# Third gate group of a fused attention and two-MLP kernel: other buffers for its logits, and other steps for its load, clamp, exponential and logarithm

## The chip, the cores and the metric

The kernel runs on one core of a Trainium2 chip. The time is device microseconds of one execution; of several runs the median is given. The profile is one execution of its own, and times in it count from the first instruction of its span.

Engines are called TensorE (PE in the rows, its weight loads PEld), VectorE (DVE), ScalarE (ACT), GpSimd (POOL) and SyncE (SP). SyncE issues nearly all DMAs. Each engine works through its own instructions in order and waits for the others by semaphores.

## The reference

Three parts feed each other; all are float32.

```python
# 1: gated linear attention; batch 4, 8 heads, 768 positions, 48 per head
f = 1.0 / (1.0 + np.exp(-f_logit))
for t in range(S):
    state = f[:, :, t, :, None] * state + np.einsum('bhd,bhe->bhde', k[:, :, t], v[:, :, t])
    y[:, :, t] = np.einsum('bhd,bhde->bhe', q[:, :, t], state)
# 2: MLP on the 3072 tokens of 384 values, 2048 wide
h = x @ w_in
x = (h * (1.0 / (1.0 + np.exp(-h)))) @ w_out
# 3: 8 experts, one for each token, 1024 wide
logits = x @ w_gate
e = argmax(logits); gate_w = softmax(logits)[e]
out = gate_w * (np.maximum(x @ w1[e], 0.0) @ w2[e])
```

The inputs q, k and v are normal numbers times 0.1, f_logit is normal times 0.5 plus 2.

## The kernel before

**Chunks and groups.** The 3072 tokens are 24 chunks of 128, six to a batch. A chunk goes through the attention alone, with a state carried from chunk to chunk. Chunks make groups of 2, 2, 3, 3, 3, 3, 3, 3 and 2; a group goes through the first MLP together. Group 2 is chunks 4 to 6, group 3 is chunks 7 to 9.

**The gates of a group.** For each chunk the logits f are loaded ([128, 384] floats), clamped from below on VectorE (`f_step` 0), and turned into log(1 + exp(-f)) on ScalarE: an exponential (step 1) and a logarithm (step 2), in place. ScalarE needs another table of functions for the logarithm than for the exponential and for the tanh of the MLP, so it loads one ahead of the logarithm, and the pinned step `table` loads the old one back. From group 2 on, the logits of a whole group stand in one tile `in_f` of three chunks, with one buffer, and each of the three operations is one instruction over it (`f_group`). `att0(n)` casts a chunk's logarithms to two float32r parts, lfh and lfl, for groups whose `n` is 7 or more; a running sum over the chunk, `pl`, follows on TensorE.

**Steps.** The main loop runs over steps `s`, one for each block of 128 of the 2048 hidden columns of a group: `moe_h` (nine matmuls into ph, ScalarE's tanh se, VectorE's product sg), `moe_g` (high and low part, gh on ScalarE and gl on VectorE), and `moe_o` of two steps earlier (matmuls with gh and gl into px, which hold a group's result). The steps of groups 0 and 1 are 0 to 31, those of group 2 begin at 32, of group 3 at 48. ph has two banks, so a step's ph needs the sg of two steps before. When a group is done, `moe_x2` copies px into tiles x2 (five buffers of 388 floats), first for group 0 in step 32 and group 1 in step 33. Those rows wait there for the expert choice and its scatter.

**The order written out by hand.** For steps 0 to 30 the list `STEPS` gives three strings a step: what goes ahead of `moe_h`, what goes between `moe_h` and `moe_g`, and what goes behind `moe_o`. These names are mapped to functions by `do`; for the first 31 steps every instruction that they issue is pinned to this order on its engine. Behind that, a scheduler orders instructions.

The names that matter here:

- `li`, `lo`: load a block of w_in or w_out; `ci0` to `ci2`, `co0` to `co2`: three VectorE operations that make float32 numbers of the float64 that is loaded (cv); `hi`, `ho` and `Li`, `Lo`: its high part on ScalarE and its low part on VectorE. The two sets are about six steps ahead of the step that needs them.
- `f`: load of a chunk's logits; `fclamp`, `fexp`, `flog`: `f_group` of a group; `table`: the other table back.
- `fk`, `fq`, `kt`, `qt`: transposes of k and q on TensorE and their copies, on ScalarE for chunks below 7; `sc`: the scores; `am`: their mask, on VectorE; `past`, `own`: the parts of y from the earlier state and from the chunk itself; `pu`, `st`: the state; `y`: y's copy from PSUM.
- `yd`: `y_turn`. Chunks 4, 5 and 6 (`TURN`) leave y turned; three DMAs write it to DRAM, and one reads it back in the form that the MLP takes. All four are issued by SyncE one behind the other, so the last waits for the landing of the first three. `xh`, `xl` read the tile y.

The other pieces of the kernel, from chunk 7 on, are put at slots by a plan (`plan`, `after`): `att0(7)`, `att0(8)`, `att0(9)` at steps 27, 32 and 37, the load of the next group's logits at step 41.

Of the kernel before, what the change touches and what calls it, by code (L numbers as in the profile page):

```python
# [9 lines left out]
F32 = mybir.dt.float32  # L10
# [11 lines left out]
P = 128  # L22
CAP = 512
ROW = 388
# [90 lines left out]
def kernel(  # L115
# [15 lines left out]
    B, H, S, D = q.shape  # L131
    NT, DM = out.shape
    DFF = moe_w_in.shape[1]
    E, _, F2 = moe2_w1.shape
    KC = DM // P
# [7 lines left out]
    sizes = [2, 2] + [CPG] * ((NCH - 6) // CPG) + [2]  # L143
    NG = len(sizes)
    starts = [sum(sizes[:g]) for g in range(NG)]
# [13 lines left out]
    att = phase.enter_context(tc.tile_pool(name="att", bufs=1))  # L159
# [5 lines left out]
    ends = dram.tile([NCH, DM], F32, name="ends")  # L165
    xs = dram.tile([E * CAP, ROW], F32, name="xs")
    ys = {n: dram.tile([NPR * P, P], F32, name=f"ys_{n}") for n in TURN}
# [22 lines left out]
    def turned(n):  # L190
        return n > 6 or n in TURN
# [11 lines left out]
        return dict(tag=other, bufs=BUFS[other]) if n == 1 else dict(tag=own)  # L203

    fb = {}

    def load_chunk(n, names, pin=lambda fn: fn):
        b, c = divmod(n, CPB)
        g, r = group_of[n]
        for nm in names:  # L210
            src = {"f": f_logit, "q": q, "k": k, "v": v}[nm]
            if nm == "v":
                tag, bufs = ("gl", GB) if n == 1 else ("in_v", 1)
                flat = att.tile([P, H * D + 16], F32, tag=tag, name=f"v_{n}", bufs=bufs)
                if turned(n):
                    nc.gpsimd.memset(flat[:, H * D :], 0.0)
                t = flat[:, : H * D].rearrange("p (h d) -> p h d", h=H)
                loaded[nm, n] = flat
            elif n == 1:
                tag = {"f": "sg", "q": "gh", "k": "gh"}[nm]  # L220
                t = att.tile([P, H, D], F32, tag=tag, name=f"{nm}_{n}", bufs=BUFS[tag])
            elif nm == "f":
                if n in F_HOME:
                    fb[g] = att.tile([P, 1, H, D], F32, tag=F_HOME[n], name=f"f_{n}")
                elif n == starts[g]:
                    fb[g] = att.tile([P, CPG, H, D], F32, tag="in_f", name=f"f_{n}")
                t = fb[g][:, r if g > 1 else 0]
            else:
                t = att.tile([P, H, D], F32, tag="in_" + nm, name=f"{nm}_{n}")
            (pin(nc.sync.dma_start) if not strict else sy.dma_start)(out=t, in_=src[b, :, c * P : (c + 1) * P, :].rearrange("h p d -> p h d"))  # L230
            loaded.setdefault((nm, n), t)
# [13 lines left out]
    ve, ac, sy = Pinned(nc.vector), Pinned(nc.scalar), Pinned(nc.sync)  # L245
# [140 lines left out]
    am = {}  # L386
    ysb = {}
    xt = {}

    def f_step(t, k):  # L390
        if k == 0:
            ve.tensor_scalar_max(t, t, FMIN)
        elif k == 1:
            ac.activation(t, t, AF.Exp, scale=-1.0)
        else:
            ac.activation(t, t, AF.Ln, bias=1.0)

    def f_group(g, k):
        f_step(fb[g][:, : sizes[g]], k)

    def att0(n):
        f = loaded.pop(("f", n))
# [39 lines left out]
    def exps(n, nm):  # L442
        t = att.tile([P, H, D], F32, name=f"{nm}_{n}", **first_use(n, nm, "se"))
        scale = 1.0 if nm == "en" else -1.0
        ac.activation(t.rearrange("p h d -> p (h d)"), pls[n][:, :DM], AF.Exp, scale=scale)
        ee[nm, n] = t
# [10 lines left out]
    def put_ends(n, eng):  # L457
        ep2 = ee["ep", n].rearrange("p h d -> p (h d)")
        eng.dma_start(out=ends[n : n + 1, :], in_=ep2[P - 1 : P, :])
# [20 lines left out]
    def flat(n, nm):  # L480
        pads, i = (qpads, 1) if nm == "q" else (kpads, 2)
        p = use(n, i, f"p{nm}_{n}")
        for r in range(NPR):
            pe.transpose(
                p[:112, r * P : (r + 1) * P],
                pads[n % 2][:, 2 * r : 2 * r + 2, :].rearrange("p h d -> p (h d)")[:, :112],
                ident,
            )
        bd[nm, n] = p

    def unflat(n, nm):
        t = att.tile([112, NPR, P], F32, tag=nm + "t", name=f"{nm}t_{n}", bufs=2)
        p3 = bd.pop((nm, n))[:112, :].rearrange("p (r t) -> p r t", r=NPR)
        (nc.vector.tensor_copy if nm == "k" and n >= KACT else ac.copy)(t, p3)
        bd[nm + "t", n] = t
# [93 lines left out]

    def y_turn(n):  # L590
        yt = ysb[n]
        y = ysb[n] = att.tile([P, KC, P], F32, tag="y", name=f"y_{n}")
        if n in TURN:
            rows = ys[n].rearrange("(r p) t -> p r t", r=NPR)
            sy.dma_start(out=rows[:112, :2], in_=yt[:112, :2])
            for k in range(2):
                sy.dma_start(out=rows[64 * (1 - k) : 64 * (1 - k) + D, 2:], in_=yt[64 * k : 64 * k + D, 2:])
            sy.dma_start(out=y, in_=ys[n].rearrange("(h x) t -> h x t", h=H)[:, :D])
            return
        for h in range(H):  # L600
            r, j = divmod(h, 2)
            k = j ^ r // 2
            sy.dma_start(out=y[h * P // H : (h + 1) * P // H], in_=yt[64 * k : 64 * k + D, r])

    def att4(n):
        if n % CPB:
            y_past(n)
        y_own(n)
        if n % CPB < CPB - 1:
            gain(n)  # L610
        y_out(n)
        if turned(n):
            y_turn(n)
        if n % CPB < CPB - 1:
            carry(n, bd.pop(("pu", n)), n % CPB == 0)

    def carry(n, pu, first):
        pu3 = pu.rearrange("p (r e) -> p r e", r=NPR)
        ab = a_all[:112, n, :, None].to_broadcast([112, NPR, D])
        s = packed_state[:112, :, :D]  # L620
        if first:
            ve.tensor_tensor(out=s, in0=pu3, in1=ab, op=ALU.mult)
        else:
            ve.tensor_tensor(out=s, in0=pu3, in1=s, op=ALU.add)
            ve.tensor_tensor(out=s, in0=s, in1=ab, op=ALU.mult)
# [83 lines left out]
    x2 = {}  # L709
# [624 lines left out]
    for n in range(NCH):  # L1334
        g, r = group_of[n]
# [74 lines left out]
    def queue(early):  # L1410
        return ac if early else sy

    do = dict(
        f=lambda n: load_chunk(n, "f"), k=lambda n: load_chunk(n, "k"), q=lambda n: load_chunk(n, "q"),
        v=lambda n: load_chunk(n, "v"), clamp=lambda n: f_step(loaded["f", n], 0),
        exp=lambda n: f_step(loaded["f", n], 1), log=lambda n: (f_step(loaded["f", n], 2), set_f(n)),
        fclamp=lambda g: f_group(g, 0), fexp=lambda g: f_group(g, 1), flog=lambda g: f_group(g, 2), lf=set_f,
        table=lambda n: ac.preload_act_table_set("exp_and_others"),
        pl=sums, en=lambda n: exps(n, "en"), ep=lambda n: exps(n, "ep"), kmul=kmul, qmul=qmul,
        fk=lambda n: flat(n, "k"), fq=lambda n: flat(n, "q"), kt=lambda n: unflat(n, "k"), qt=lambda n: unflat(n, "q"),  # L1420
        sc=scores, am=mask, pu=gain, st=lambda n: carry(n, bd.pop(("pu", n)), n % CPB == 0), past=y_past, own=y_own,
        y=y_out, yd=y_turn, pt=flip_y, xh=x_high, xl=x_low,
        ends=lambda n: put_ends(n, queue(n == 0)), a=lambda n: spread_ends(n, queue(n == 0)),
        w=lambda n: warm(spare_bank[0], n),
    )
# [33 lines left out]
    g = NG - 1  # L1459
# [8 lines left out]
    def preload():  # L1468
# [6 lines left out]
        g=rest_fetch, t=lambda: turn(items["rest"]),  # L1475
# [50 lines left out]
```

## Time and profile before

| | before |
|---|---|
| median of 3 runs | 825.18 us (819.7 to 825.69) |
| the profiled execution's own time | 824.64 us |
| its span, first to last instruction | 822.9 us |
| TensorE busy | 799.7 us, 97% of the span |
| VectorE busy | 467.7 us, 57% |
| ScalarE busy | 379.1 us, 46% |
| mean granted clock of TensorE | 0.989 |

The profiled execution's time is 1.7 us longer than its span: what lies around the first and the last instruction. Shares of busy time are averages over the span; the stretch of the pinned steps looks otherwise, for example VectorE is busy for 4.93 of the 5 us from 95 to 100 us. Matmuls are pipelined and their ends are modelled, so a busy TensorE isn't TensorE at its peak.

### The profile page before, as it was taken

What the parts mean: (1) busy time and instruction counts of PE and PEld (TensorE: products, weight loads), DVE (VectorE), ACT (ScalarE), POOL (GpSimd) and SP (SyncE); (2) the same over time, 40 slices, a digit from 0 to 9 for tenths busy, and PEclk for the clock granted to TensorE, in tenths of its full rate; (3) what the DMA queues carried; (4) which work ended last, traced back from release to release, by engine and by line L of the source; (5) the groups of instructions that cost most, each with busy time, mean ns of one, the idle gap of its engine ahead of it and who ended that gap; (6) DMA issues with size and microseconds to landing.
All of it is one profiled execution on the core that took longest, in us unless ns stands there. A gap on an engine that the chain in (4) does not pass through costs nothing.

```text
span 822.9 us, 15636 instructions
## 1 busy us (share of the span) xinstructions
PE 799.7 (97%) x5831; PEld 750.0 (91%) x5831; DVE 467.7 (57%) x1258; ACT 379.1 (46%) x838; POOL 62.4 (8%) x114
## 2 busy tenths in 40 slices
PE   7999999999999999999999999999999999999994
PEld 4889979989999999999999999999899999989994
DVE  7789986555556555646656556366573426345520
ACT  5465564453453453454345342354473526445520
POOL 2000000001000100100100101001200010111001
PEclk9799999999999999999999999999999999999998
DMA  9566686424333343343443422323380617644500
GB/s 217 150 167 161 171 242 183 112 40 116 79 87 90 92 100 83 92 107 78 107 97 79 106 58 57 119 65 119 129 278 31 205 51 259 219 151 161 172 17 29
DMA packets 173197, 100.34 MB, mean 122 GB/s; under 512 B 115507, under 2 KB 166723, under 8 KB 173110
## 3 DMA queue, kind: packets, MB, share of 16 engines
q1 hardware_dynamic: 168724, 88.56, 39.4%
q0 software_dynamic: 3280, 9.49, 3.1%
q10 hardware_dynamic: 1106, 1.18, 0.4%
q8 instruction: 48, 0.79, 0.4%
q14 instruction: 39, 0.32, 0.1%
HBM read 79.35 MB, written 16.97 MB: 117 GB/s over the span
## 4 chain that ended last, share of the span: by engine, by line
PE 78%; issue 8%; DVE 7%; DMA 2%; ACT 2%; POOL 1%; SPq 1%; POOLq 0%; ACTq 0%; DVEq 0%
PE ph L420 22%; PE px L420 21%; PE p L420 8%; PE po L420 8%; PE py L420 4%; PE sc L420 2%; DVE out_cv L248 2%; PE pyb L420 2%; DVE in_cv L248 1%; PE plt L425 1%; PE pl L420 1%; PE p_r L420 1%; POOL out_dram L988 1%; PE pq L425 1%; PE pxs L425 1%
## 5 line engine op out<-in xcount | busy, mean ns | idle before, releaser
L420 PE MATMUL px<-out_lo,gh 128*128 128x384 f32 x368 | 130.2, 354 | 0.0
L679 DVE SCALAR_TENSOR_TENSOR sg<-se,ph 128x384 f32<-128x384 f32 (+1 forms) x113 | 60.2, 532 | 116.0 <-ACT se L677 114.9
L420 PE MATMUL ph<-xth,in_lo 128*128 128x384 f32 (+1 forms) x384 | 123.9, 323 | 0.7 <-DVE sg L679 0.5
L420 PE MATMUL px<-out_hi,gl 128*128 128x384 f32 x368 | 124.0, 337 | 0.0
L420 PE MATMUL ph<-xth,in_hi 128*128 128x384 f32 (+1 forms) x384 | 123.6, 322 | 0.0
L420 PE MATMUL ph<-xtl,in_hi 128*128 128x384 f32 (+1 forms) x384 | 122.3, 325 | 1.3 <-DVE sg L248 1.2
L420 PE MATMUL px<-out_hi,gh 128*128 128x384 f32 x368 | 123.4, 335 | 0.0
L677 ACT ACTIVATE se<-ph 128x384 f32<-128x384 f32 (+1 forms) x113 | 53.6, 474 | 137.1 <-PE ph L420 131.6
L687 ACT CAST gh<-sg 128x384 fp32r<-128x384 f32 (+1 forms) x113 | 56.3, 499 | 53.1 <-DVE sg L679 50.7
L688 DVE TENSOR_TENSOR gl<-sg,gh 128x384 fp32r<-128x384 f32 (+1 forms) x113 | 60.4, 535 | 25.8 <-ACT gh L687 25.1
L420 PEld LDWEIGHTS ph<-xtl,in_hi 128*128 128x128 f32 x384 | 71.7, 188 | 3.2 <-DVE sg L248 1.9
L420 PEld LDWEIGHTS ph<-xth,in_lo 128*128 128x128 f32 x384 | 72.2, 188 | 1.5 <-DVE sg L679 0.8
L420 PEld LDWEIGHTS ph<-xth,in_hi 128*128 128x128 f32 x384 | 72.1, 188 | 0.0
L420 PEld LDWEIGHTS px<-out_lo,gh 128*128 128x128 f32 x368 | 69.1, 188 | 2.5 <-ACT gh L687 0.6
L420 PEld LDWEIGHTS px<-out_hi,gl 128*128 128x128 f32 x368 | 69.3, 188 | 0.3
L420 PEld LDWEIGHTS px<-out_hi,gh 128*128 128x128 f32 x368 | 69.1, 188 | 0.0
L420 PE MATMUL po<-w_lo,hh 128*128 128x384 f32 (+4 forms) x184 | 62.9, 342 | 0.0
L420 PE MATMUL po<-w_hi,hh 128*128 128x384 f32 (+4 forms) x184 | 61.9, 336 | 0.0
L420 PE MATMUL po<-w_hi,hl 128*128 128x384 f32 (+4 forms) x184 | 61.9, 336 | 0.0
L276 DVE TENSOR_TENSOR w_lo<-w_raw,w_hi 128x384 fp32r<-128x384 f32 x104 | 52.3, 552 | 10.8 <-ACT w_hi L275 10.7
L420 PE MATMUL p<-xsl,w_hi 128*128 128x480 f32 (+6 forms) x168 | 58.4, 347 | 0.0
L420 PE MATMUL p<-xsh,w_hi 128*128 128x480 f32 (+6 forms) x168 | 58.3, 347 | 0.0
(290 smaller groups left out, 1532.6 us busy)
## 6 DMA issues: line engine op xcount, KB each, us to landing
w_raw<-in_moe_w_dram SPq DMA_DIRECT2D x64, 384.0 KB
xs<-big SPq DMA_DIRECT2D x8, 776.0 KB
in_again<-in_moe_w_in_dram SPq DMA_DIRECT2D x16, 384.0 KB
out_again<-in_moe_w_out_dram SPq DMA_DIRECT2D x16, 384.0 KB
in_raw<-in_moe_w_in_dram SPq DMA_DIRECT2D x15, 384.0 KB
xe<-xs SPq DMA_DIRECT2D x7, 776.0 KB
out_raw<-in_moe_w_out_dram SPq DMA_DIRECT2D x14, 384.0 KB
f<-in_f_logit_dram SPq DMA_DIRECT2D x24, 192.0 KB
```

The source lines that it names most:

```text
L248: return lambda *a, **k: tc.keep_in_program_order(fn(*a, **k))
L276: (keep(lo_engine.tensor_sub) if pin else lo_engine.tensor_sub)(lo[:, h], x, hi[:, h].bitcast(F32))
L420: ins = nc.tensor.matmul(*a, **k)
L425: ins = nc.tensor.transpose(*a, **k)
L677: ac.activation(e, ph[:, :GT], AF.Tanh, scale=0.5)
L679: ve.scalar_tensor_tensor(out=t, in0=e, scalar=1.0, in1=ph[:, :GT], op0=ALU.add, op1=ALU.mult)
L687: ac.copy(hi, t)
L688: ve.tensor_sub(lo, t, hi.bitcast(F32))
L988: ins = nc.gpsimd.indirect_dma_start(out=out[:, :], out_offset=bass.IndirectOffsetOnAxis(ap=idx[:n], axis=0), in_=o[:n], in_offset=None, b ...
```

## The change

- The loads of f_7, f_8 and f_9 go from step 18 to the end of step 5. Their tiles are no longer the group's `in_f` but three of the five x2 buffers, one tile a chunk.
- `fclamp:3` and `fexp:3` go from step 21 to step 7, `flog:3` and the `table` behind it from step 22 to step 8. `f_group(3, k)` is now three instructions, one for each chunk's tile, where it was one.
- `y_turn` is cut in two for chunks 4 to 6: the writes (`yd`) and the readback (`yb`, `y_back`). `yb` stands a step behind `yd`; `yd:5` moves from step 17 to 16, so that its readback keeps step 17.

```diff
-    ('co0:5 co1:5', 'co2:5 lo:7 ho:4 Lo:4 pt:3 xh:3 xl:3 st:3', ''),
+    ('co0:5 co1:5', 'co2:5 lo:7 ho:4 Lo:4 pt:3 xh:3 xl:3 st:3', 'f:7 f:8 f:9'),
     ('ci0:6 ci1:6', 'ci2:6 li:8 ho:5 Lo:5 pl:4 en:4 ep:4 kmul:4 qmul:4 ends:4 k:5 q:5', ''),
-    ('co0:6 co1:6', 'co2:6 lo:8 hi:6 Li:6', ''),
-    ('ci0:7 ci1:7', 'ci2:7 li:9 ho:6 Lo:6 fk:4 fq:4 kt:4 qt:4 a:4', ''),
+    ('co0:6 co1:6', 'co2:6 lo:8 hi:6 Li:6 fclamp:3', 'fexp:3'),
+    ('ci0:7 ci1:7', 'ci2:7 li:9 ho:6 Lo:6 fk:4 fq:4 kt:4 qt:4 a:4', 'flog:3 table:0'),
     ('co0:7 co1:7', 'co2:7 lo:9 hi:7 Li:7 sc:4 am:4', ''),
     ('ci0:8 ci1:8', 'past:4 ci2:8 li:10 ho:7 Lo:7', 'own:4 pu:4 y:4 v:5'),
     ('co0:8 co1:8', 'co2:8 lo:10 hi:8 Li:8 st:4 pl:5 en:5 ep:5 kmul:5 qmul:5 k:6 q:6 yd:4', ''),
-    ('ci0:9 ci1:9', 'ci2:9 li:11 ho:8 Lo:8', ''),
+    ('ci0:9 ci1:9', 'ci2:9 li:11 ho:8 Lo:8 yb:4', ''),
...
-    ('ci0:11 ci1:11', 'ci2:11 li:13 ho:10 Lo:10 xh:4 xl:4', ''),
-    ('co0:11 co1:11', 'co2:11 lo:13 hi:11 Li:11 pl:6 en:6 ep:6 kmul:6 qmul:6 ends:6 yd:5', ''),
-    ('ci0:12 ci1:12', 'ci2:12 li:14 ho:11 Lo:11 f:7 f:8 f:9', ''),
+    ('ci0:11 ci1:11', 'ci2:11 li:13 ho:10 Lo:10 xh:4 xl:4 yd:5', ''),
+    ('co0:11 co1:11', 'co2:11 lo:13 hi:11 Li:11 pl:6 en:6 ep:6 kmul:6 qmul:6 ends:6 yb:5', ''),
+    ('ci0:12 ci1:12', 'ci2:12 li:14 ho:11 Lo:11', ''),
...
-    ('co0:13 co1:13', 'co2:13 lo:15 hi:13 Li:13 sc:6 am:6 fclamp:3', 'fexp:3'),
-    ('ci0:14 ci1:14', 'ci2:14 ho:13 Lo:13 xh:5 xl:5', 'flog:3 table:0'),
+    ('co0:13 co1:13', 'co2:13 lo:15 hi:13 Li:13 sc:6 am:6', ''),
+    ('ci0:14 ci1:14', 'ci2:14 ho:13 Lo:13 xh:5 xl:5', ''),
     ('co0:14 co1:14', 'co2:14 hi:14 Li:14', ''),
     ('ci0:15 ci1:15', 'own:6 pu:6 y:6 ci2:15 ho:14 Lo:14', ''),
     ('co0:15 co1:15', 'co2:15 hi:15 Li:15 st:6 yd:6', ''),
-    ('', 'ho:15 Lo:15', ''),
+    ('', 'ho:15 Lo:15 yb:6', ''),
...
                 if n in F_HOME:
                     fb[g] = att.tile([P, 1, H, D], F32, tag=F_HOME[n], name=f"f_{n}")
+                elif g == 3:
+                    fx[n] = att.tile([P, ROW], F32, tag="x2", name=f"f_{n}", bufs=5)[:, :DM]
                 elif n == starts[g]:
                     fb[g] = att.tile([P, CPG, H, D], F32, tag="in_f", name=f"f_{n}")
-                t = fb[g][:, r if g > 1 else 0]
+                t = fx[n].rearrange("p (h d) -> p h d", h=H) if n in fx else fb[g][:, r if g > 1 else 0]
...
     def f_group(g, k):
-        f_step(fb[g][:, : sizes[g]], k)
+        for t in [fx[n] for n in range(starts[g], starts[g] + sizes[g])] if g == 3 else [fb[g][:, : sizes[g]]]:
+            f_step(t, k)
...
     def y_turn(n):
         yt = ysb[n]
-        y = ysb[n] = att.tile([P, KC, P], F32, tag="y", name=f"y_{n}")
         if n in TURN:
             rows = ys[n].rearrange("(r p) t -> p r t", r=NPR)
             sy.dma_start(out=rows[:112, :2], in_=yt[:112, :2])
             for k in range(2):
                 sy.dma_start(out=rows[64 * (1 - k) : 64 * (1 - k) + D, 2:], in_=yt[64 * k : 64 * k + D, 2:])
-            sy.dma_start(out=y, in_=ys[n].rearrange("(h x) t -> h x t", h=H)[:, :D])
             return
+        y = ysb[n] = att.tile([P, KC, P], F32, tag="y", name=f"y_{n}")
...
+    def y_back(n):
+        y = ysb[n] = att.tile([P, KC, P], F32, tag="y", name=f"y_{n}")
+        sy.dma_start(out=y, in_=ys[n].rearrange("(h x) t -> h x t", h=H)[:, :D])
```

## Rows read from the trace of the kernel before

**Rows 1.** The page, part 1: busy us (share of the span), instructions.

```profile
PE 799.7 (97%) x5831; PEld 750.0 (91%) x5831; DVE 467.7 (57%) x1258; ACT 379.1 (46%) x838; POOL 62.4 (8%) x114
```

**Rows 2.** Waits of VectorE, 28 to 135 us: us in total, times, longest.

```profile
DVE sg L248 <- ACT se L248: 9.4, 7, 2.6
```

**Rows 3.** Timeline of ScalarE, 98 to 126 us: start us, us, instruction.

```profile
107.90 1.17 ACT L248 ACTIVATE f<-f 128x1152 f32<-128x1152 f32 x1 [2.40 <-DVE f L248]
...
110.47 1.28 ACT L248 ACT_TABLE_LOAD   x1
111.77 1.17 ACT L248 ACTIVATE f<-f 128x1152 f32<-128x1152 f32 x1
112.95 1.28 ACT L248 ACT_TABLE_LOAD   x1
114.25 0.38 ACT L248 ACTIVATE se<-ph 128x256 f32<-128x256 f32 x1
```

**Rows 4.** Timeline of VectorE, 98 to 126 us; in brackets the idle time before.

```profile
107.12 0.75 DVE L248 TENSOR_SCALAR f<-f 128x1152 f32<-128x1152 f32 x1
107.78 0.42 DVE L248 TENSOR_TENSOR gl<-sg,gh 128x256 fp32r<-128x256 f32 x1
...
109.37 0.42 DVE L248 SCALAR_TENSOR_TENSOR sg<-se,ph 128x256 f32<-128x256 f32 x1 [0.31 <-ACT se L248]
...
114.66 0.42 DVE L248 SCALAR_TENSOR_TENSOR sg<-se,ph 128x256 f32<-128x256 f32 x1 [2.26 <-ACT se L248]
```

**Rows 5.** Timeline of TensorE, 107 to 125 us.

```profile
109.84 0.39 PE L420 MATMUL ph<-big,in_hi 128*128 128x256 f32 x1 [0.45 <-DVE sg L248]
...
115.14 0.38 PE L420 MATMUL ph<-xtl,in_hi 128*128 128x256 f32 x1 [1.24 <-DVE sg L248]
...
122.59 0.28 PE L420 MATMUL ph<-big,in_hi 128*128 128x256 f32 x1
...
124.70 0.28 PE L420 MATMUL ph<-xtl,in_hi 128*128 128x256 f32 x1
```

**Rows 6.** The tile f, its clamps in the pinned steps: duration ns min/median/max.

```profile
L248 DVE TENSOR_SCALAR f<-f x6: 349/356/753, 5.2 to 107.1; 128x384 f32<-128x384 f32 x4, 128x1152 f32<-128x1152 f32 x2
```

**Rows 7.** Timeline of ScalarE, 55 to 82 us.

```profile
58.16 0.50 ACT L248 ACTIVATE en<-pl 128x384 f32<-128x384 f32 x1
58.55 0.50 ACT L248 ACTIVATE ep<-pl 128x384 f32<-128x384 f32 x1
...
62.66 0.38 ACT L248 ACTIVATE se<-ph 128x256 f32<-128x256 f32 x1
...
63.81 0.61 ACT L248 COPY qt<-pq 112x512 f32<-112x512 f32 x1
```

**Rows 8.** Timeline of VectorE, 55 to 82 us.

```profile
63.16 0.42 DVE L248 TENSOR_TENSOR gl<-sg,gh 128x256 fp32r<-128x256 f32 x1
...
66.83 0.41 DVE L248 SCALAR_TENSOR_TENSOR sg<-se,ph 128x256 f32<-128x256 f32 x1
...
68.10 1.28 DVE L248 TENSOR_TENSOR am<-sc,trir 128x512 f32<-128x512 f32 x2
...
74.58 0.42 DVE L248 SCALAR_TENSOR_TENSOR sg<-se,ph 128x256 f32<-128x256 f32 x1 [1.54 <-ACT se L248]
```

**Rows 9.** Timeline of TensorE, 62 to 74 us.

```profile
65.17 1.16 PE L420 MATMUL sc<-qt,kt 48*128 48x128 f32 x16
...
68.84 0.43 PE L420 MATMUL py<-qt,state 48*64 48x128 f32 x4 [0.19 <-DVE am L248]
```

**Rows 10.** Timeline of SyncE, 48 to 126 us: DMAs that it issues.

```profile
55.80 0.35 SPq L248 DMA_DIRECT2D out_raw<-in_moe_w_out_dram  x1
...
100.16 3.72 SPq L248 DMA_DIRECT2D f<-in_f_logit_dram  x3
```

**Rows 11.** Engines in stretches: busy us (instructions), granted clock, DMA share, GB/s.

```profile
19.40:29.60 10.20, 10.15 (x60) 8.58 (x60) 4.54 (x10) 4.57 (x10) 0.00 (x0) 0.50 0.48 145
110.00:115.20 5.20, 3.96 (x48) 3.45 (x48) 2.90 (x8) 5.05 (x8) 0.41 (x1) 1.00 0.78 282
```

More of the change, by code (lines that the diff above doesn't have):

```diff
@@ L205 @@
     fb = {}
+    fx = {}
     def load_chunk(n, names, pin=lambda fn: fn):
@@ L1421 @@
         sc=scores, am=mask, pu=gain, st=lambda n: carry(n, bd.pop(("pu", n)), n % CPB == 0), past=y_past, own=y_own,
-        y=y_out, yd=y_turn, pt=flip_y, xh=x_high, xl=x_low,
+        y=y_out, yd=y_turn, yb=y_back, pt=flip_y, xh=x_high, xl=x_low,
         ends=lambda n: put_ends(n, queue(n == 0)), a=lambda n: spread_ends(n, queue(n == 0)),
```

## Prediction

> **What bounds the kernel now.** I read the page first: TensorE is busy for 97% of the span [rows 1], so no other engine can give back more than some per cent, and only where TensorE stands still. The change touches the first 31 steps, which run in a fixed order on every engine, so I read that stretch (about 30 to 130 us) alone: who VectorE waits for, then ScalarE, VectorE and TensorE in order of time. I number a step by its place in STEPS and count the activations se (one a step) to know which step a row belongs to. In this stretch VectorE, not TensorE, ends last most of the time: it does three conversion operations, a low part, sg and gl in each step and hardly rests. It rests for ScalarE's se, 9.4 us in seven waits [rows 2]; no wait in that answer names a DMA, so no load is late. Two of the seven belong to the group's logits.
>
> **The old place, steps 21 to 23.** VectorE runs the clamp at 107.12, 0.75 us, and its next operation starts at 107.78: 0.66 us spent. ScalarE then runs the exponential (1.17 us) ahead of that step's se, so VectorE rests 0.31 us before sg at 109.37. At the end of step 22 ScalarE loads a table, takes the logarithm and loads the table back, without a break between them: 110.47 to 114.23, 3.76 us, with the next se at 114.25 [rows 3]. VectorE rests 2.26 us for that se, to 114.66 [rows 4]. Together 0.66 + 0.31 + 2.26 = 3.23 us of VectorE's time.
>
> TensorE shows less, 0.45 us before 109.84 and 1.24 us before 115.14 [rows 5], 1.7 us in all. That isn't its whole loss: its three steps from 115.14 to the ph at 122.59 take 7.45 us, 2.48 each, by sg, while the next, without a wait, takes 2.11, to 124.70 [rows 5]. So VectorE decides until about step 27, and TensorE takes over there. If VectorE is 3.23 us earlier, TensorE's own work still fits: from the end of step 23's ph at about 107.8 to the ph at 122.59 it has nine blocks, each half of such a 2.11 us step (four ph, five px), and own and pu of chunk 6, by estimate 1.5 us, 11 us in all, which would end at 118.8; the last sg that it needs would be there at about 118.7, VectorE's 3.23 us earlier. Taking the work away gives back **3.2 us**; the bounds are 1.7 us (the visible rests alone) and 3.3 us.
>
> **The new place, steps 7 to 9.** The sequence stands at the same points: clamp in the middle of step 7 just ahead of gl, exponential at its end, logarithm and table at the end of step 8. It is now three tiles, so three instructions for one each time. A clamp of 128x384 takes 0.35 us against 0.75 for the large form [rows 6]; with VectorE's overlap, as above, three cost about 0.78 us against 0.66. Two 128x384 exponentials of another tile start 0.39 us apart [rows 7], so three take 1.17 us to the next start, against 1.07 from the large one. Splitting thus costs 0.1 us an operation, and lets the first exponential start after the first clamp, which gives 0.4 us back.
>
> Now ScalarE's chain, forward. The clamp takes the place of the gl at 63.16 [rows 8]; first clamp done 63.52, exponentials from 63.55, three times 0.39: se of step 8 at 64.72 instead of 62.66 [rows 7]. Behind it stand in this step what the old place hadn't: the copies kt and qt of chunk 4. qt begins 1.15 us after se, so 65.87, and ends at about 66.4 (0.61 us long, the next starts some 0.5 later); gh, 0.4 long, then to 66.8. Table 1.28, three logarithms 1.17 and the tail of the last some 0.15, table 1.28: 66.8 to 70.7. se of step 9 is at 70.74, sg 0.4 later at 71.14, as 114.25 and 114.66 stand to each other. VectorE alone would have come to that sg at 66.83 + 0.78 = 67.6, so it rests some 3 us here and about half a microsecond ahead of gl of step 8. The masks am of chunk 4 follow sg by 1.27 us [rows 8], at 72.41 instead of 68.10: **4.3 us late**.
>
> Who waits for that: TensorE's y of the earlier state in step 10. Before, it already waited for am by 0.19 us, at 68.84 [rows 9]; so am decides, and all that TensorE has behind it (px, own and pu of chunk 4, ph of step 11) comes 4.3 us later. That ph is what VectorE rests for at 74.58 (1.54 us) [rows 8], so no rest is left there to swallow the delay; both engines go on 4.3 us late. TensorE stands still for about 1.25 us ahead of the scores of step 9, which it began at 65.17 [rows 9] and which need qt, and, with the scores, px and ph between them, some 3.1 us ahead of the y. The trace of before doesn't show the sequence at this place. From the rows the cost lies between 1.7 us, the rests that the same sequence showed on TensorE at the old place, and 4.3 us; I take 4.3, because the row nearest to it, the y that waits for am, leaves no slack.
>
> **Loads and turns.** The three loads of f go from step 18 to step 5. Their buffers have had no user, so SyncE issues them at once behind the load at 55.80 (done at 56.15). In before they took 3.72 us to issue from 100.16 [rows 10], and VectorE read them at 107.12, 7.0 us after the first issue, without a wait; now it is 56.15 to 63.16, 7.0 us again. Hidden; at most some half a microsecond late. What they push back on SyncE (a load of an in piece, ends, k and q) is read four steps later or more. The three buffers belong to results that are first written at steps 32 and 33, after the casts of f_7 and f_8, and f_9 gives its buffer back at step 37, before the third group's results: no new wait.
>
> y_turn and y_back: SyncE now issues the readback of a turned chunk a step after the writes, so it needn't stand at their landing. Every piece keeps several steps of lead (the readbacks of steps 12, 17 and 26 are read in steps 16, 22 and 30), and no engine waits for a load, so I take nothing for it. The bounds are a gain of 0.3 us and a loss of 0.3 us, the order of the smaller rests seen here. The removed loads at step 18 free SyncE where no engine was waiting for it: nothing.
>
> **The sum.** 4.3 - 3.2 = +1.1 us on the profiled execution's 824.64: 825.7. The median of the runs is 0.5 us above that execution, so 826.
>
> **Rivals.**
> *The new rest is partly covered, slightly faster.* If TensorE is held only as long as it visibly was at the old place, 1.7 us: 824.64 + 1.7 - 3.2 = 823.1. If the 1.54 us that VectorE rests at 74.58 absorb a part: 824.2. For it: TensorE shows hardly a rest in this stretch, so it might run ahead. Against: the y waits for am already [rows 9], and TensorE works in order.
>
> *The clock falls, slower.* TensorE would stand still for 4.4 us of the 8.5 us from 65.2 to 73.7, and the matmuls of the y that end this rest are small. In before the granted clock fell to its lower level (0.50, 1.2 GHz) at 19.4 and stayed there to 29.6, after a stretch of small matmuls with rests; it stayed at 1.00 from 110.0 to 115.2 although TensorE was busy for only 3.96 of 5.2 us [rows 11]. My new rest is longer than the second case. If the clock falls at about 74 for as long as in the opening, 10.2 us, half of that is lost, 5.1 us, because TensorE is what ends last from there to step 11 and again from step 14: 825.7 + 5.1 = 830.8. If it comes back sooner, since large matmuls follow at once, some 828. It decides from the point where TensorE's rest ahead of the y is long enough for a 0.50 to show; with a rest as at the old place it doesn't.
> The Trainium skill (TensorE: Matmul & The Clock Gate, section "Why this matters for your kernels") warns against idle gaps between bursts of matmuls, since the clock drops back to half. It speaks against this change, as the row of the opening does; by that rule the time is the 830.8 of this rival, by the row of 110.0 to 115.2 it is 825.7.
>
> *The logits aren't there in time.* The change wouldn't do what it says if the load landed after 63.16; the clamp would hold VectorE, and am with it. The margin is that of before, so it costs 0 to 2 us: up to 827.7.
>
> **How the numbers follow.** The forecast, 824.5 to 827: 0.50. Covered, 822 to 824.5: 0.22. Clock, 827.5 to 831: 0.18. Late logits, or another order of the work after step 31, which isn't fixed: 0.10, on both sides. The range reaches from 821 (the covered case, and runs of before that lie up to 5.5 us under their median) to 831. About 1%, 8.3 us, is what a measurement of this kernel tells from no change (its three runs alone span 6 us); no case reaches it by itself, so faster by over 1% gets 0.04, slower 0.05, within 0.91.
>
> **What would show it.** In the changed kernel: no f instruction and no table load from 105 to 120 us, with sg at an even pace there (right), or a rest that stays (wrong). At 63 to 74 us: three clamps, three exponentials, two table loads around three logarithms; VectorE resting about 3 us for se of step 9; TensorE resting ahead of the scores and of the y. If that y comes at about 73, the 4.3 us stand; at 71 or earlier, I have overrated it. Granted clock 1.00 from 65 to 90 refutes the second rival. VectorE waiting for a DMA at the clamp would prove the third. I would be wrong in sign if the two places cost the same, which the copies kt and qt on ScalarE's path speak against.

## The result and the profile after

The changed kernel takes 826.96 us (median of 11 executions) where the kernel before, measured beside it, takes 820.94 us: ratio 1.0076, 95% interval 1.0056 to 1.0097. It is 6.0 us, 0.8%, slower. The forecast was 826 us, in a range of 821 to 831, and no change of more than 1%: the time came out in the range, but its effect was forecast as +1.1 us. The two don't go together because the sum started too high, from the profiled execution's 824.64 us. That execution is one of those whose granted clock fell in the opening, for 10.2 us [rows 11]; step 7 begins 5.1 us later in it than in the profile of the third experiment below, which has no such fall. In six of the nine profiles of the table below step 7 begins at about 55 us instead of 60 (two of the other three are late for a load at about 48 us, not for the opening), and the median of more executions of the kernel before is 820.94. One execution of all that follow, of the kernel with the sequence in steps 9 and 10, was slow, 874.35 us at a mean granted clock of 0.85, and its ratio leaves it out.

The profiled execution of the changed kernel takes 828.93 us, with a span of 827.1 us. The page, part 1, busy us and share of the span:

```profile
PE 800.4 (97%) x5831; PEld 750.6 (91%) x5831; DVE 468.3 (57%) x1260; ACT 379.2 (46%) x842; POOL 62.6 (8%) x114
```

Nothing shows there: TensorE has the same work as in [rows 1]. So the stretch of the pinned steps is read again, first the new place. ScalarE and VectorE, steps 7 to 9 (start us, us, instruction, in brackets the idle time before):

```profile
59.39 1.36 ACT L251 ACTIVATE f<-f 128x384 f32<-128x384 f32 x3 [0.80 <-DVE f L251]
60.65 0.36 ACT L251 ACTIVATE se<-ph 128x256 f32<-128x256 f32 x1
...
61.79 0.59 ACT L251 COPY qt<-pq 112x512 f32<-112x512 f32 x1
...
62.71 1.28 ACT L251 ACT_TABLE_LOAD   x1
64.00 1.35 ACT L251 ACTIVATE f<-f 128x384 f32<-128x384 f32 x3
65.37 1.28 ACT L251 ACT_TABLE_LOAD   x1
66.67 0.38 ACT L251 ACTIVATE se<-ph 128x256 f32<-128x256 f32 x1
```

```profile
59.00 0.89 DVE L251 TENSOR_SCALAR f<-f 128x384 f32<-128x384 f32 x3
...
67.08 0.42 DVE L251 SCALAR_TENSOR_TENSOR sg<-se,ph 128x256 f32<-128x256 f32 x1 [3.07 <-ACT se L251]
...
68.36 1.28 DVE L251 TENSOR_TENSOR am<-sc,trir 128x512 f32<-128x512 f32 x2
...
77.29 0.42 DVE L251 SCALAR_TENSOR_TENSOR sg<-se,ph 128x256 f32<-128x256 f32 x1 [3.99 <-ACT se L251]
```

Three clamps, three exponentials, the logarithms between two table loads, and kt and qt between them and the se of step 8, as forecast. Against [rows 7, 8] the masks am move from 1.27 us behind an undisturbed sg to 1.28 us behind one that waited 3.07 us. VectorE's rest ahead of the sg of step 11, 1.54 us in [rows 8], is now 3.99 us. TensorE:

```profile
62.44 1.16 PE L424 MATMUL sc<-qt,kt 48*128 48x128 f32 x16 [1.33 <-ACT qt L251]
...
69.10 0.69 PE L424 MATMUL py<-qt,state 48*64 48x128 f32 x4 [3.19 <-DVE am L251]
```

It rests 1.33 us ahead of the scores and 3.19 us ahead of the earlier-state y, where it rested 0.19 us in [rows 9]. The y starts at 69.10 us and not at the 73 of the forecast, but step 7 begins 4.1 us earlier in this execution: counted from step 7's se (56.09 here, 60.23 before) the y comes after 13.0 us instead of 8.6, so it is 4.4 us late. And from the end of that rest on the clock is low. Engines in stretches, TensorE's busy us first, the granted clock third from the end:

```profile
65.90:69.10 3.20, 0.01 (x2) 0.00 (x1) 2.02 (x5) 2.63 (x6) 0.00 (x0) 0.87 0.07 9
68.30:75.00 6.70, 5.90 (x44) 4.83 (x46) 4.93 (x12) 0.73 (x2) 0.00 (x0) 0.50 0.39 117
75.20:80.00 4.80, 4.80 (x42) 4.48 (x39) 2.68 (x7) 2.88 (x9) 0.11 (x1) 1.00 0.37 81
...
109.30:112.60 3.30, 3.30 (x14) 2.85 (x13) 2.26 (x6) 3.27 (x4) 0.00 (x0) 0.50 0.97 319
```

From 68.3 to 75.1 us it is 0.50, its lower level, and again from 109.2 to 112.6 us. The second belongs to the old place, which isn't empty. SyncE, VectorE, ScalarE and TensorE there:

```profile
96.85 1.28 SPq L233 DMA_DIRECT2D f<-in_f_logit_dram  x2
...
101.15 0.46 SPq L233 DMA_DIRECT2D f<-in_f_logit_dram  x1
```

```profile
106.31 0.76 DVE L395 TENSOR_SCALAR f<-f 128x1152 f32<-128x1152 f32 x1 [3.48 <-DMA f<-in_f_logit_dram]
...
111.48 0.43 DVE L251 TENSOR_TENSOR gl<-sg,gh 128x256 fp32r<-128x256 f32 x1 [1.01 <-ACT gh L251]
...
113.17 0.42 DVE L251 SCALAR_TENSOR_TENSOR sg<-se,ph 128x256 f32<-128x256 f32 x1 [0.41 <-ACT se L251]
```

```profile
107.10 1.16 ACT L397 ACTIVATE f<-f 128x1152 f32<-128x1152 f32 x1 [3.55 <-DVE f L395]
...
108.69 1.28 ACT L399 ACT_TABLE_LOAD   x1
109.98 1.16 ACT L399 ACTIVATE f<-f 128x1152 f32<-128x1152 f32 x1
...
111.46 1.28 ACT L251 ACT_TABLE_LOAD   x1
112.76 0.39 ACT L251 ACTIVATE se<-ph 128x256 f32<-128x256 f32 x1
```

```profile
108.39 0.45 PE L424 MATMUL spare<-out_hi,gl 128*128 128x384 f32 x1 [1.80 <-DVE gl L251]
...
116.12 0.45 PE L424 MATMUL spare<-out_hi,gl 128*128 128x384 f32 x1 [1.00 <-DVE gl L251]
```

The clamp, exponential and logarithm of a whole group stand here again, 1152 wide, but by their lines (L395, L397 and L399 instead of L251) they are not pinned, and their loads (L233) neither: they are the fourth group's, chunks 10 to 12. The tile f tells where they came from. Its clamps that aren't pinned, in before and in the changed kernel (first and last start in us):

```profile
L392 DVE TENSOR_SCALAR f<-f x5: 560/759/761, 161.4 to 429.5; 128x1152 f32<-128x1152 f32 x4, 128x768 f32<-128x768 f32 x1
```

```profile
L395 DVE TENSOR_SCALAR f<-f x5: 561/760/762, 106.3 to 434.3; 128x1152 f32<-128x1152 f32 x4, 128x768 f32<-128x768 f32 x1
```

The first of five moved from 161.4 us, in step 39, to 106.3 us, between the se of step 20 and that of step 21. The third group's logits used to keep the only buffer in_f until step 37. Now in_f is free as soon as the second group's sums are done, so the scheduler, which may place unpinned instructions among the pinned ones, put the fourth group's loads on SyncE at 96.85 us and its clamp on VectorE ahead of pinned work, and there VectorE stands 3.48 us for the load. VectorE's waits from 28 to 135 us, which named no DMA in [rows 2]:

```profile
DVE sg L251 <- ACT se L251: 13.0, 7, 4.0
DVE f L395 <- DMA f<-in_f_logit_dram: 3.5, 1, 3.5
```

### The profile page after: what moved, and what is told of

Read it like the earlier page. It is cut to its first block, busy times and chain, and to the rows that moved or that the text cites. A ratio compares the mean times of both kernels' runs of the same rounds, so it can differ in the third digit from the quotient of the medians.

```text
span 827.1 us, 15637 instructions
## 1 busy us (share of the span) xinstructions
PE 800.4 (97%) x5831; PEld 750.6 (91%) x5831; DVE 468.3 (57%) x1260; ACT 379.2 (46%) x842; POOL 62.6 (8%) x114
## 4 chain that ended last, share of the span: by engine, by line
PE 76%; issue 7%; DMA 6%; DVE 4%; ACT 3%; SPq 1%; POOL 1%; POOLq 0%; ACTq 0%; DVEq 0%
PE ph L424 22%; PE px L424 21%; PE po L424 7%; PE p L424 7%; PE py L424 4%; PE sc L424 3%; DMA w_raw<-in_moe_w_dram 2%; PE pyb L424 2%; PE pl L424 1%; PE spare L424 1%; DMA f<-in_f_logit_dram 1%; PE plt L429 1%; POOL out_dram L995 1%; PE p_r L424 1%; PE pq L429 1%
```

## The experiments

Ratios are to the kernel before, measured beside each of them; its medians there are 819.45 to 819.74 us, 1.2 to 1.5 us under the 820.94 above, so differences of medians from different experiments are good to a microsecond or two. A ratio is not simply the quotient of two medians. To see where time goes, I set the starts of se (one a step, ScalarE's timeline) of the profiled executions beside each other. The kernel of the third experiment serves as the measure: from step 5 to step 36 its profile runs 5.05 to 5.10 us ahead of before's, and it has no low clock in the opening. Each entry is the time between two starts, and the difference to that kernel in parentheses:

| kernel | step 7 to 11 | step 20 to 27 | span |
|---|---|---|---|
| before | 60.23 to 74.17: 13.94 | 100.47 to 122.24: 21.77 | 822.9 |
| before, split readback | 55.16 to 69.09: 13.93 | 95.39 to 117.14: 21.75 | 817.9 |
| changed | 56.09 to 76.87: 20.78 (+6.85) | 103.18 to 127.34: 24.16 (+2.41) | 827.1 |
| changed, fourth group pinned | 55.39 to 75.06: 19.67 (+5.74) | 101.35 to 119.69: 18.34 (-3.41) | 818.4 |
| changed, 20 matmuls | 55.09 to 73.44: 18.35 (+4.42) | 99.74 to 122.37: 22.63 (+0.88) | 819.8 |
| changed, 50 matmuls | 59.77 to 77.58: 17.81 (+3.88) | 103.89 to 126.39: 22.50 (+0.75) | 825.4 |
| changed, pinned and 50 matmuls | 54.61 to 72.94: 18.33 (+4.40) | 99.25 to 117.59: 18.34 (-3.41) | 816.6 |
| pinned, sequence in steps 9 and 10 | 60.73 to 77.00: 16.27 (+2.34) | 103.69 to 122.02: 18.33 (-3.42) | 820.8 |
| the same, later loads | 54.97 to 71.30: 16.33 (+2.40) | 98.00 to 116.34: 18.34 (-3.41) | 815.5 |

**The fourth group kept in program order.** The edit, in the changed kernel:

```diff
-                at(s0, load_chunk, m, "f")
+                at(s0, load_chunk, m, "f", *([keep] if g == 4 else []))
...
-    def f_step(t, k):
+    def f_step(t, k, pin=False):
+        hold = keep if pin else lambda fn: fn
         if k == 0:
-            ve.tensor_scalar_max(t, t, FMIN)
+            hold(ve.tensor_scalar_max)(t, t, FMIN)
...
-            f_step(t, k)
+            f_step(t, k, g == 4)
```

(The exponential and the logarithm likewise.) Expected:

> The changed kernel, with the load, clamp, exponential and logarithm of the fourth group (chunks 10 to 12) kept in program order, so that they can't move ahead into the pinned steps. Theory A, the freed buffer: the third group's logits left the one buffer in_f early, so the scheduler drew the fourth group's load, clamp and table loads into steps 20 to 22, where VectorE waited 3.5 us for the load. Then this kernel shows no f instruction from 100 to 130 us, the se of steps 20 and 27 keep or narrow their distance to before by 3.2 us instead of widening it by 2.4, and the time falls by about 4.7 us against the changed kernel, to 822 us. Theory B, the rest there comes of something else in the pinned order (the split readbacks, or TensorE's own work): the time stays at 826 to 827 us.

Measured: 820.76 us, ratio 0.9997 (0.9971 to 1.0024). VectorE has no f instruction from 100 to 130 us, and steps 20 to 27 give back 3.41 us where the changed kernel lost 2.41. Theory A holds, B falls: keeping one group's logits from moving ahead takes off 826.96 - 820.76 = 6.2 us by the medians. Program order puts the fourth group's clamp at 180.3 us, later than before's 161.4 us, so the edit does more than undo the move; the last experiment below shows what that alone is worth. The masks of step 9 and the clock are as they were: TensorE rests 3.2 us and the clock is 0.50 from 68.6 to 72.0 us in this profile.

```profile
PE py L425 <- DVE am L251: 3.5, 2, 3.2
PE sc L425 <- ACT qt L251: 2.1, 2, 1.3
```

```profile
65.20:68.50 3.30, 0.11 (x3) 0.11 (x4) 2.12 (x5) 2.62 (x6) 0.00 (x0) 1.00 0.10 12
68.60:71.90 3.30, 3.28 (x22) 2.49 (x18) 3.27 (x9) 0.40 (x1) 0.00 (x0) 0.50 0.29 106
72.00:80.00 8.00, 8.00 (x79) 7.53 (x78) 5.02 (x14) 3.30 (x10) 0.11 (x1) 1.00 0.55 147
```

**The buffers alone.** The kernel before with the x2 tiles and the three instructions, at the old steps. The edit is the lines of the change's diff that have to do with `fx` and `f_group`; STEPS and `y_turn` are as before.

> The kernel before with one part of the change alone: the third group's logits in three x2 buffers and three instructions for one, at their old steps 18, 21 and 22; y_turn as before. Theory A: the freed in_f alone draws the fourth group's logits into the pinned steps, so this kernel pays for both groups there, and is about 5 us slower than before (826 us), with an f instruction of 128x1152 between 95 and 110 us. Theory B: the buffers alone do nothing, 821 us as before.

Measured: 821.26 us, ratio 1.0019 (0.9987 to 1.0052), not to be told from before; the time is nearer to theory B's. The mechanism of theory A is there all the same, since VectorE runs both groups in the pinned steps:

```profile
93.11 0.75 DVE L395 TENSOR_SCALAR f<-f 128x1152 f32<-128x1152 f32 x1
...
98.22 0.43 DVE L251 TENSOR_TENSOR gl<-sg,gh 128x256 fp32r<-128x256 f32 x1 [1.82 <-ACT gh L251]
...
104.86 0.89 DVE L251 TENSOR_SCALAR f<-f 128x384 f32<-128x384 f32 x3
...
112.37 0.42 DVE L251 SCALAR_TENSOR_TENSOR sg<-se,ph 128x256 f32<-128x256 f32 x1 [2.46 <-ACT se L251]
```

but without a wait for a load, at a price of 3.15 us from step 17 (87.20 against 87.52 us) to step 27 (119.97 against 117.14), and 1.4 us of it come back later, in the profile between steps 39 and 42, where the fourth group's logits no longer stand. The 5 us were too much: I took them from the changed kernel, where the wait for the load and the low clock are in them.

**The readback alone.** The kernel before with `y_back` and the moved `yd` and `yb`; the edit is those lines of the change's diff and nothing else.

> The kernel before with the other part alone: the writes of the turned chunks and their readback apart by a step. No engine waits for these loads, so by the prediction's step it does nothing: within 0.3 us of before. If SyncE's stand at the landing had cost something, it is up to 1 us faster; if the readback of chunk 6 now comes too late, up to 1 us slower, with a rest of ScalarE ahead of xth at about 128 us.

Measured: 819.63 us, ratio 0.9981 (0.9947 to 1.0014). It does nothing that can be told, as forecast.

**Matmuls in TensorE's rest.** In the changed kernel, 20 matmuls with a constant operand ahead of the y of step 10, into columns 384 to 511 of a result bank, which nobody reads:

```diff
-    ('ci0:8 ci1:8', 'past:4 ci2:8 li:10 ho:7 Lo:7', 'own:4 pu:4 y:4 v:5'),
+    ('ci0:8 ci1:8', 'z:20 past:4 ci2:8 li:10 ho:7 Lo:7', 'own:4 pu:4 y:4 v:5'),
...
+        z=lambda n: [pe.matmul(px[0][0][:, DM:512], ones, ones, start=False, stop=False) for _ in range(n)],
```

> The changed kernel with 20 matmuls of 128 columns more on TensorE ahead of the earlier-state y of step 10, where TensorE rests 3.2 us for the masks am; their results land in columns of a result bank that nobody reads. Theory C, the clock: the rest lets the granted clock fall to 0.50 from 68 to 75 us, which costs 2.4 us; with the matmuls it stays at 1.00 there and the time is about 2.4 us less, 824.5 us. Rival: the steps after 10 are late for the masks alone; the clock may stay up, but the time stays at 827 us or grows by what the matmuls take beyond the rest.

Measured: 825.9 us, ratio 1.0062 (1.0026 to 1.0098), between the two expectations and by its median undecided, since the executions lie between 820.77 and 832.18: four with a mean granted clock of 0.993 or more take 823.2 us or less, eight with 0.991 or less take 825.3 us or more. The profiled one is of the first kind; its clock is 1.00 from 15 to 135 us, and it loses 4.42 us from step 7 to 11, not 6.85. Twenty matmuls leave 2.1 us of the rest, so the next two experiments took 50.

**Both.** The pinned fourth group and 50 matmuls:

> The changed kernel with both: the fourth group's logits kept in program order, and 50 matmuls of 128 columns (20 in the run before) ahead of the earlier-state y of step 10, whose results nobody reads. Theory C, the clock: the granted clock stays at 1.00 from 60 to 80 us, step 7 to step 11 loses 4.4 us instead of the 5.7 that it lost with the pinned group alone, and the executions whose clock doesn't fall in the opening are 1.3 us faster than that kernel's, 818.5 us. Rival: the matmuls take as much as the clock did: 820 us.

Measured: 818.13 us, ratio 0.9969 (0.9947 to 0.9991), 0.3% under before. Steps 7 to 11 lose 4.40 us. TensorE at the place of the rest, and the clock there:

```profile
60.95 1.16 PE L425 MATMUL sc<-qt,kt 48*128 48x128 f32 x16 [1.34 <-ACT qt L251]
...
64.26 2.96 PE L425 MATMUL px<-ones 128*128 128x128 bf16 x50
67.62 0.44 PE L425 MATMUL py<-qt,state 48*64 48x128 f32 x4 [0.39 <-DVE am L251]
```

```profile
64.80:68.00 3.20, 2.81 (x48) 2.44 (x45) 2.40 (x5) 2.25 (x6) 0.00 (x0) 1.00 0.14 31
68.00:75.00 7.00, 6.84 (x75) 6.04 (x74) 5.38 (x14) 2.91 (x8) 0.11 (x1) 1.00 0.44 129
```

Between this kernel and the one with the pinned group alone lie 1.34 us of these steps by the profiles (5.74 and 4.40) and 2.6 us by the medians. The mean granted clock of the executions says the same: 0.994 or more in ten of twelve here, in one of twelve there. The rival falls. That the kernel is now faster than before isn't due to the change alone: the kernel before with the same group pinned (the last experiment) takes 819.08 us, ratio 0.9983, and the two intervals overlap. What is left, 4.4 us, is the wait for am itself: the matmuls are done in the rest and the y comes no sooner.

**The 50 matmuls alone.** The changed kernel without the pinning:

> The changed kernel with the 50 matmuls ahead of the earlier-state y of step 10 and nothing else: the fourth group's logits move ahead as in the changed kernel. Against the kernel with both edits it shows what the freed buffer costs when the clock is held at the new place: theory A says steps 20 to 27 lose 0.9 to 2.4 us where that one gains 3.4, less about 1 us that comes back behind step 32, so 821.5 to 823.5 us against its 818.1. Against the changed kernel it shows what the clock at the new place costs by the median: 3 to 5 us. Rival: the clock falls at the other rest, for the fourth group's load at about 105 us, in most executions anyway, and the median stays over 825.

Measured: 823.34 us, ratio 1.0045 (1.0015 to 1.0074). The time is in theory A's range, and the rival falls. Against the changed kernel the matmuls are worth 826.96 - 823.34 = 3.6 us by the medians, 2.5 us by the ratios, whose intervals overlap. Not all of that lies at the new place: in the profiles steps 7 to 11 lose 3.88 us instead of 6.85, and steps 20 to 27 lose 0.75 us instead of 2.41; there the clock doesn't fall a second time, and the load is waited for more briefly. The fourth group's logits cost 823.34 - 818.13 = 5.2 us with the clock held, of which 0.75 + 3.41 = 4.2 us show in steps 20 to 27. VectorE waits for their load for 1.8 us in this profile, 3.5 us in the changed kernel's:

```profile
DVE f L395 <- DMA f<-in_f_logit_dram: 1.8, 1, 1.8
```

The profiled execution takes 827.11 us, more than the median, because TensorE waits 2.0 us for v of chunk 3 in it, to 47.6 us, and the clock is at 0.50 from 48.8 to 55.6 us.

**Another place, beside the second group's.** Loads in step 2, clamp, exponential and logarithm in step 4, where the second group's logarithm stands:

```diff
-    ('am:3 co0:4 co1:4', 'past:3 co2:4 li:7 ho:3 Lo:3 xh:2 xl:2', 'flog:2 table:0 lf:4 lf:5 lf:6 own:3 pu:3 y:3 v:4'),
+    ('am:3 co0:4 co1:4', 'past:3 co2:4 li:7 ho:3 Lo:3 xh:2 xl:2 fclamp:3', 'fexp:3 flog:2 flog:3 table:0 lf:4 lf:5 lf:6 own:3 pu:3 y:3 v:4'),
```

> The changed kernel with the fourth group kept in program order and the third group's sequence beside the second's: loads at the end of step 2, clamp in step 4, exponential and logarithm at its end with the second group's logarithm, so that one pair of table loads serves both. It costs 1.2 us for the exponentials, 1.2 for the logarithms and 0.8 for the clamps at most, against 4.4 us at steps 7 to 9. If table loads and the copies kt and qt make the price of the new place, step 3 to step 11 loses 2.5 us or less against before and the time is 2 us under before's. Rival: the steps there are as tight for ScalarE (it is busy from 50 to 55 us), so it loses 4 us or more and ends as before.

Measured: 821.76 us, ratio 1.0013 (0.9988 to 1.0037). It missed for a reason that neither side had: a load. TensorE waits for v of chunk 3, and the clock falls behind it (0.50 from 49.6 to 59.9 us):

```profile
49.96 0.66 PE L425 MATMUL py<-v,am 128*128 128x48 f32 x2 [4.39 <-DMA v<-in_v_dram]
```

SyncE had issued the three loads of f for 3.2 us ahead of v. v was issued at 44.68 us, and its first matmul starts 5.3 us later. In the profile of the 50 matmuls alone v was issued at 42.30 us, its first matmul starts 5.3 us later as well, and the wait is 2.0 us. So the loads of f explain some 2.4 us of the 4.39; the rest is the late v that other kernels show without them. The shared table load was not tested.

**Another place, steps 9 and 10.** With the fourth group pinned:

```diff
-    ('co0:7 co1:7', 'co2:7 lo:9 hi:7 Li:7 sc:4 am:4', ''),
-    ('ci0:8 ci1:8', 'past:4 ci2:8 li:10 ho:7 Lo:7', 'own:4 pu:4 y:4 v:5'),
+    ('co0:7 co1:7', 'co2:7 lo:9 hi:7 Li:7 sc:4 am:4 fclamp:3', 'fexp:3'),
+    ('ci0:8 ci1:8', 'past:4 ci2:8 li:10 ho:7 Lo:7 flog:3 table:0', 'own:4 pu:4 y:4 v:5'),
```

> The changed kernel with the fourth group kept in program order and the third group's clamp behind the masks am of step 9, its exponential at the end of step 9, its logarithm in step 10 ahead of gh. If the price of the new place is that am, and with it the earlier-state y, comes late, this place is cheap: TensorE has y, own, pu and a ph to do while ScalarE loads its tables, and step 7 to step 11 loses about 2.2 us instead of 4.4, with no rest of TensorE ahead of that y; the time is 2 us under before's. Rival: what counts is ScalarE's 3.8 us ahead of any se, so it loses 4 us here as well and ends as before.

Measured: 818.18 us, ratio 0.9971 (0.9945 to 0.9997). Steps 7 to 11 lose 2.34 us, as expected, and TensorE's rest ahead of the y is gone:

```profile
69.32 0.44 PE L425 MATMUL py<-qt,state 48*64 48x128 f32 x4 [0.17 <-DVE am L251]
...
77.17 0.91 PE L425 MATMUL pl<-f,trir 128*128 128x384 f32 x2 [2.61 <-ACT yt L251]
```

A new rest of 2.61 us comes later, ahead of the sums of step 11, for yt on ScalarE. It lies just behind the se of step 11, so the table's interval leaves it out: from step 7 to step 20 this kernel loses 2.73 us, where the one with the pin and 50 matmuls loses 4.41. Behind am the same 3.8 us of tables and logarithm on ScalarE thus cost some 2.7 us instead of 4.4. In the profiled execution TensorE also waited 2.0 us for v of chunk 3 at 48 us, with a low clock behind it.

**The same with later loads.** f:7 to f:9 at the end of step 7 instead of step 5:

> The kernel with the sequence in steps 9 and 10 and the fourth group kept in program order, with the third group's loads two steps later, at the end of step 7. If the loads of step 5 play no part in the wait of 2.0 us for v of chunk 3 that the profile of the kernel before it showed at 48 us (v is issued ahead of them), nothing changes: step 7 to step 11 loses 2.3 us against before, steps 20 to 27 give back 3.4, and the time is 1 to 3 us under before's, 817 to 819 us. If they do, the slow executions of that kernel go, and the median is under 817.5. Should the loads now come too late for the clamp at 69 us, VectorE shows a wait for them and the time is over 820.

Measured: 819.88 us, ratio 1.0002 (0.9976 to 1.0029). Steps 7 to 11 lose 2.40 us (2.80 to step 20) and steps 20 to 27 give back 3.41, and no instruction waits for the loads; the profiled execution has the shortest span of all, 815.5 us. The median isn't lower than with the early loads. The loads of step 5 can't be what made v late in the kernel before this one, since SyncE issued them only behind that wait, which ended at 48.02 us:

```profile
43.30 0.40 SPq L251 DMA_DIRECT2D v<-in_v_dram  x1
...
56.69 2.61 SPq L251 DMA_DIRECT2D f<-in_f_logit_dram  x3
```

What does make it late stays open.

**The kernel before with the fourth group pinned.** None of the change:

> The kernel before with nothing of the change, and the fourth group's load, clamp, exponential and logarithm kept in program order. It tells how much of what the pinned kernels get back behind step 32 comes of the pinning alone: 1 to 2 us faster than before if the rest of 1.0 us that TensorE has at 170 us in before, for the fourth group's logarithm, goes; as before otherwise.

Measured: 819.08 us, ratio 0.9983 (0.9961 to 1.0006): no difference that can be told by the times. In the profile the distance to the kernel with the split readback goes from +0.55 us in step 30 to -0.84 us in step 42, so about 1.4 us come back there, in the profile alone. Program order puts the fourth group's clamp at 178.6 us here, where before it stood at 161.4 us.

## Why the prediction was right and wrong

**The new place: right, in mechanism and size.** The step "4.3 us late", with TensorE resting some 1.25 us ahead of the scores and 3.1 us ahead of the y, measured 1.33 and 3.19 us, and 4.4 us from step 7 to step 11 where the clock is held. The row that settled it was the small wait of the y for am [rows 9]; the kernel with the sequence behind am shows the reverse side, 2.7 us up to step 20 instead of 4.4.

**The old place: the size right, the use wrong.** "Taking the work away gives back 3.2 us": where it really is taken away, it gives back 3.41 or 3.42 us, in each of the table's four profiles with the fourth group pinned. TensorE's visible rests of 1.7 us would have been the wrong measure. In the changed kernel the place was filled again, and steps 20 to 27 lost 2.41 us. The step that failed is in "Loads and turns": "no new wait". It followed the buffers that the logits moved into, and who needs them next. It didn't ask who had been held back by the buffer that they left, though the kernel's description says it: in_f has one buffer, the next group's logits are planned for step 41, and nothing behind the first 31 steps is pinned. The wait that disappeared was the one on in_f, and it had kept another group's table loads out of the tight steps. "The removed loads at step 18 ... nothing" fell with it, since other loads took their place. The prediction gave "another order of the work after step 31" a part of 0.10; the order did change, but before step 31.

**The clock: the rival came true as well, not instead.** The granted clock fell behind the rest of 3.19 us, for 6.8 us in the changed kernel's profile and 3.4 us in the pinned one's, and cost 2.45 and 1.3 us of steps 7 to 11. That is less than the 5.1 us of the rival as long as in the opening, and about its shorter form ("some 828", 2.3 us above the forecast). The fall at 109.2 us, at the fourth group's logits, the rival didn't have. The 50 matmuls in the rest, which do nothing else, kept the clock at 1.00. The Trainium skill's warning against idle gaps between bursts of matmuls (TensorE: Matmul & The Clock Gate, section "Why this matters for your kernels") agrees with this rest: 3.2 us, then 0.50. The length of a rest alone doesn't tell it here, though: TensorE's 2.61 us in the kernel with the sequence in steps 9 and 10 left the clock at 1.00, while its 2.05 us for v, in the same profile, were followed by 0.50.

**Covered, and late logits: neither.** VectorE's clamps of the third group wait for nothing at 59.00 us. The readback did nothing, as forecast.

**The sum.** By profiles against the kernel with the split readback: 0.9 us before step 7 (the opening differs between executions by as much), +4.4 for am, +2.45 for the clock, +2.41 in steps 20 to 27 where -3.2 was forecast, and -1.0 behind step 32, where the fourth group's logits are now missing: 9.2 us, as the spans say (827.1 and 817.9). By medians it is 6.0 us; the changed kernel's profiled execution lies 2.0 us above its median.

With both side effects held, the two places come out as forecast: in the kernel with the pin and 50 matmuls steps 7 to 27 take 54.61 to 117.59, 62.98 us, and in the kernel before with the same pin 55.70 to 117.69, 61.99 us. That is +1.0 us, where the sum had +1.1. For the changed kernel itself, that the time came out in the range was luck: the base was 4.2 us too high (825.18 as the median, 820.94 with more executions), and the effect was forecast 4.9 us too small. What stays open is why v of chunk 3 is late in some executions.

## What to carry to other kernels

A tile that moves to another buffer gives its old buffer free, and the next user of the old one may then run earlier, in front of work that is tight: follow both buffers, and pin what the old wait had been holding. What a step costs in a tight stretch is decided by who waits behind it there, so the same 3.8 us on one engine cost 4.4 us ahead of the masks and some 2.7 us behind them. Take the base of a sum from several executions, and look at their granted clock before a profile is taken as the normal case.

## What the runs showed of the hardware

In the pinned steps the granted clock fell to 0.50 at rests of TensorE of 1.80, 2.0, 3.2 and 4.39 us and stayed low for 3.4 to 10.2 us; the same rest of 3.2 us, in the changed kernel and in the one with the pinned group, was followed by 6.8 us in one profile and 3.4 us in the other. A rest of 2.61 us, in the kernel with the sequence in steps 9 and 10, left it at 1.00:

```profile
74.60:77.10 2.50, 0.00 (x0) 0.00 (x0) 0.50 (x2) 2.47 (x6) 0.00 (x0) 1.00 0.71 188
```

Fifty matmuls of 128 columns with a constant operand, 2.96 us long, held it at 1.00 at the place of the 3.2 us rest, in both profiles that have them.

SyncE issued the changed kernel's fourth-group loads with other DMAs between them, the first at 96.85 us and the last at 101.15 us, and VectorE had to wait until 106.3 us. Three loads of the same size that it issued together, from 52.05 to 54.73 us, were there at 59.00 us without a wait. The DMA share of the two stretches is 0.80 (96.8 to 106.3 us) and 0.96 (52 to 59 us), so the DMA engines were no busier where the loads came late. That the spread of their issue made them late is likely, but no run tests it.
